# Retention and two matrix products on one core: states of the first six chunks as 64x64 blocks, and another order of the opening

## The chip, the cores and the metric

The kernel runs on one core of a Trainium2 chip. The metric is the time of one execution on the device in microseconds (us). A core has TensorE (PE in the profile; PEld is its weight load), VectorE (DVE), ScalarE (ACT), GpSimd (POOL) and SyncE (SP), which issues most of the transfers. Each engine has its own queue of instructions, works it off in order, and waits on semaphores for the others.

## The reference, cut to what matters

```python
def _attn_ref(q, k, v):                      # each 4 x 8 x 768 x 64
    gamma = 1.0 - 2.0 ** (-5.0 - np.arange(H))
    for t in range(S):
        state = gamma * state + k[:, :, t] (outer) v[:, :, t]     # 64 x 64 for each head
        y[:, :, t] = scale * q[:, :, t] @ state

def _moe_ref(x, w_in, w_out):                # x is 3072 x 512, made from y
    h = x @ w_in                             # 512 x 2048
    sp = np.where(h > 20.0, h, np.log1p(np.exp(np.minimum(h, 20.0))))
    return (h * np.tanh(sp)) @ w_out         # 2048 x 512
```

There are four batches, eight heads of width 64 and 768 steps in each sequence.

## The kernel before, in words

**Chunks.** The recurrence is done in chunks of 128 steps, six in a batch, 24 in all. For a chunk, the present part of y comes from scores (k times q, masked by a triangle with decay built into the scaled q and v), and the past part from the state at the end of the chunk before it (q times state). The state of a head is a 64x64 block: the sum of k-outer-v over the chunk (tile `u_ps`), plus the old state, times a decay factor for the chunk.

**How the states lie.** In chunks 0 to 4 of the first batch a pair of heads shares one full 128x128 matmul: k of two heads as weights, v of two heads as data. That gives a 128x128 block with the two wanted 64x64 blocks on its diagonal and two unwanted blocks beside them. So the state tile `st` is 128x4x128 (four pairs), and the factor tile `gcm` (L83, L105 to L108) is of that size, with the decay on the diagonal blocks and zeros elsewhere, so that one multiplication on DVE decays the state and clears the unwanted blocks (`state_first` L306, `decay_wide` L458). A past term (`past_first` L324, `past` L462) is then one full matmul for a pair of heads. From the second batch on the states are compact: 128x4x64 (`stc`), written by quarter or half-array matmuls (`outer` L425) and multiplied by the broadcast of a 128x4 tile (`gcv`).

**Blocks.** Rows of x are worked in blocks: the first of four chunks (512 rows, `first_block` L846), then blocks of two chunks. For each block, x times w_in goes to `h_ps`, through the activation on ACT, and then times w_out. Later blocks use a scheme with seven products instead of eight (`g1_seven`, `seven`). The order of all work on every engine is written out by hand: the program order is the order in each queue, and a wait on TensorE holds back whatever stands behind it.

**The opening** (`first_block`, L856 to L910). Its four chunks come as two sets of two chunks; in a set, a token pair lies in one partition, so that each half of the 64 partitions is one chunk. q is scaled on DVE, turned on TensorE and copied to `qfirst_t`. Each half (four heads) of k is cast to fp16 on ACT (`cast_two`, L248), turned by four transposes on TensorE (`turn_two`, L262) and copied from PSUM to SBUF on ACT (`turned_two`, L267). v is cast and scaled on POOL (L251). Scores are 64x64 quarter matmuls (L280), then masked on DVE (L287). The present terms are quarter matmuls too (L319). `spin` and `spin_wide` (L385, L390) are matmuls whose result is not used; the array is kept working with them. After the present and past terms of chunks 2 and 3, `xt_out` (L331) copies y to x, and `first_g1` (L842) begins x times w_in: 16 matmuls for chunks 0 and 1, then 16 for chunks 2 and 3. The state of chunk 3 (L299, L309 and L311 again) follows before the next group (L537).

**Chunks 4 and 5** are worked inside `first_g2` (L961), the second product of the first block. `outer_wide` (L448) makes the sum for chunk 4, adds the state of chunk 3, and `decay_wide` the decay; `y_two` (L511) makes the present and past terms of both chunks.

PSUM tiles come from two pools: tag `mm` has four buffers (turned halves, state sums, `h_ps`, `o_ps`), tag `at` two (scores, `y_ps`). A buffer is written again when its last reader has finished.

Of the kernel before, what the change touches and what calls it, by code (L numbers as in the profile page):

```python
# [16 lines left out]
def kernel(  # L17
# [9 lines left out]
    nc = tc.nc  # L27
# [52 lines left out]
    vs_two = qvs[:, (2 + CPB) * H:].rearrange("p (r h) -> p h r", r=R)  # L80
    ident = cpool.tile([P, P], FP16, name="ident")
    tri = cpool.tile([P, C], FP32, name="tri")
    gcm = cpool.tile([P, HP, P], FP32, name="gcm")  # L83
    gcv = cpool.tile([P, HP], FP32, name="gcv")
    warm = cpool.tile([P, 1], FP32, name="warm")
    gate_t = cpool.tile([P, 1], FP16, name="gate")
    nc.gpsimd.memset(ident, 0.0)
# [17 lines left out]
    nc.vector.memset(gcm, 0.0)  # L105
    for h in range(H):
        o = 64 * (h % 2)
        nc.vector.memset(gcm[o:o + 64, h // 2, o:o + 64], float(gamma[h] ** C))  # L108
        o = 64 * (h // HP)
        nc.vector.memset(gcv[o:o + 64, h % HP:h % HP + 1], float(gamma[h] ** C))  # L110
    decay = gcv.unsqueeze(2).broadcast_to((P, HP, D))

    win_ap = moe_w_in.rearrange("(bp p) f -> p bp f", p=P)
    wout_ap = moe_w_out.rearrange("(fb p) c -> p fb c", p=P)
# [4 lines left out]
    loaded, cast, qkts, ats, ams, states, us, ys, sus = {}, {}, {}, {}, {}, {}, {}, {}, {}  # L119
# [149 lines left out]
    def toks(c):  # L269
        return slice(c * HB, (c + 1) * HB)  # L270
# [19 lines left out]
            tri_first.rearrange("p r t -> p (r t)").unsqueeze(1).broadcast_to(  # L290
                (P, HP, R * C)), op=ALU.mult)

    def outer_first(s, chunks=(0, 1)):
        u_ps = {c: mmps.tile([P, HP, P], FP32, name="u_ps", tag="mm") for c in chunks}
        for i in range(HP):
            half, j = divmod(i, HP // 2)
            for r in range(R):
                for c in chunks:
                    nc.tensor.matmul(  # L299
                        u_ps[c][:, i], k16s[s][toks(c), half, r, 2 * j:2 * j + 2],  # L300
                        v16s[s, half][toks(c), r, 2 * j:2 * j + 2],
                        start=i == 0 and r == 0, stop=r == R - 1, skip_group_check=True)
        for c in chunks:
            us[2 * s + c] = u_ps[c]

    def state_first(g):  # L306
        u = us.pop(g)
        if g > 0:
            nc.tensor.matmul(u, ident, states[g - 1], start=False, stop=True, skip_group_check=True)  # L309
        states[g] = stp.tile([P, HP, P], FP16, name="st")  # L310
        nc.vector.tensor_tensor(states[g], u, gcm, op=ALU.mult)  # L311

    def present_first(s, y, pairs):
        for i in pairs:
            half, j = divmod(i, HP // 2)
            for r in range(R):
                for c in range(2):
                    for hh in range(2):
                        nc.tensor.matmul(  # L319
                            y[64 * hh:64 * hh + 64, c, i], v16s[s, half][toks(c), r, 2 * j + hh],  # L320
                            amf[s, half][toks(c), hh, j, r], start=i == 0 and r == 0,
                            stop=s == 0 and c == 0 and r == R - 1, skip_group_check=True)

    def past_first(g, y):  # L324
        for i in range(HP):
            nc.tensor.matmul(
                y[:, g % 2, i], states[g - 1][:, i], qfirst_t[:, i, g * C:(g + 1) * C],
                start=False, stop=True, skip_group_check=True)

    def xt_out(g, y):  # L330
        nc.scalar.copy(xts[0][:, g:g + 2], y)  # L331
# [113 lines left out]
            stcs[g] = stp.tile([P, HP, D], FP16, name="stc", tag="stc")  # L445
            by.tensor_tensor(stcs[g], sus.pop(g), decay, op=ALU.mult)

    def outer_wide(g):  # L448
        _, k16, v16, _ = cast[g]
        u_ps = u_tile()[:, 0]  # L450
        for i in range(HP):
            nc.tensor.matmul(
                u_ps[:, i], k16[:, 2 * i:2 * i + 2], v16[:, 2 * i:2 * i + 2],
                start=True, stop=True)
        sus[g] = stp.tile([P, HP, P], FP32, name="su", bufs=1)
        nc.vector.tensor_tensor(sus[g], u_ps, states[g - 1], op=ALU.add)

    def decay_wide(g):  # L458
        states[g] = stp.tile([P, HP, P], FP16, name="st")
        nc.vector.tensor_tensor(states[g], sus.pop(g), gcm, op=ALU.mult)  # L460

    def past(g, y):  # L462
        qt = qkts[g][0]
        if g < NCH:
            for i in range(HP):
                nc.tensor.matmul(
                    y(i), states[g - 1][:, i], qt[:, i], start=False, stop=True,
                    skip_group_check=True)
# [377 lines left out]
    def first_block():  # L846
        qf = load_first_q()
        for s in range(2):
            for nm in "kv":
                for half in range(2):  # L850
                    load_two(nm, s, half)
        nload[0] = CPB
        load_weights()
        xts[0] = xtp.tile([P, CPB, HP, C], FP16, name="xt")

        at = at_tile()  # L856
        spin_wide(at, HP)
        spin_wide(at, HP)
        spin(at, 8)
        tq = turn_first_q(qf, 0)  # L860
        spin_wide(at, 3)
        first_q_out(0, tq, nc.scalar)
        tq = [tq, turn_first_q(qf, 1)]
        cast_two("k", 0, 0)
        turn_two(0, 0)
        first_q_out(1, tq[1], nc.vector)
        turned_two(0, 0)
        cast_two("k", 0, 1)
        spin_wide(at, 3)
        scores_half(0, 0, at)  # L870
        mask_half(0, 0, at)
        turn_two(0, 1)
        turned_two(0, 1)
        for half in range(2):
            cast_two("v", 0, half)
        at = at_tile()
        spin_wide(at, 3)
        scores_half(0, 1, at)
        mask_half(0, 1, at)
        cast_two("k", 1, 0)  # L880
        turn_two(1, 0)
        turned_two(1, 0)
        cast_two("k", 1, 1)
        outer_first(0)
        state_first(0)
        at = at_tile()
        scores_half(1, 0, at)
        mask_half(1, 0, at)
        y = atps.tile([P, 2, HP, C], FP32, name="y_ps", tag="at")
        present_first(0, y, range(HP))  # L890
        turn_two(1, 1)
        turned_two(1, 1)
        state_first(1)
# [67 lines left out]
    def first_g2():  # L961
# [68 lines left out]
            mm(px[p], a(p, 1, 2), t(4))  # L1030
        for p in pairs:
            mm(px[p], a(p, 1, 1), b(1, 0))
        outer_wide(CPB)
        casts(CPB + 2)
        turn_by_dma(CPB + 2)
        load_q(CPB + 4)
        scores_one(CPB + 1)
        decay_wide(CPB)

        def end(p, i, half):  # L1040
            for f in range(2 * half, 2 * half + 2):
# [126 lines left out]
```

## Time and profile before

| what | value |
|---|---|
| median of three runs | 199.25 us (199.11 to 199.26) |
| profiled execution | 199.32 us |
| its span on the core | 197.5 us |
| busy: TensorE, DVE, ACT, POOL | 190.2, 142.5, 105.6, 92.9 us |
| state multiplies of the opening (L311) | four of 684 ns each |
| state matmuls of the opening (L299) | 32, 1.9 us busy |
| first block matmul (L842) | starts at 18.02 us |

The span runs from the first to the last instruction on the core; the rest of the time of an execution lies around it. A row of the timeline reads: start, duration, engine, source line, operation, output<-inputs, sizes, count; a count above one means that like instructions were merged. In square brackets stands how long the engine was idle before it and what ended that. Matmuls are pipelined: one starts while the one before it is still passing through the array, so the distance between starts tells the pace, and a duration holds some 0.2 us of latency. In the busy times by stretches the last three columns are the granted TensorE clock, the share of busy transfer engines and GB/s.

### The profile page before, as it was taken

To read this page: it belongs to the slowest core of one execution; us is meant where nothing else is said; L and a number is where in the kernel's file an instruction comes from. 1 tells how busy PE (TensorE), PEld (TensorE's weight loads), DVE (VectorE), ACT (ScalarE), POOL (GpSimd) and SP (SyncE) were. 2 spreads that over 40 slices of the span, in tenths; PEclk is the share of its full clock that TensorE was granted. 3 is DMA by queue.
4 is the path that set the end of the run, shared out by engine and by line. 5 is a ranking of instruction groups with operands and counts; after the bars stand their busy time and mean duration, and the time that the engine had idled before them with its cause. 6 is when DMAs were issued, how large, how long until landed. Compare 5 with 4: busy or idle time off the path is not lost.

```text
span 197.5 us, 5915 instructions
## 1 busy us (share of the span) xinstructions
PE 190.2 (96%) x2463; PEld 158.2 (80%) x2463; DVE 142.5 (72%) x295; ACT 105.6 (53%) x193; POOL 92.9 (47%) x129
## 2 busy tenths in 40 slices
PE   6899999999999999999999999999999999999992
PEld 2357646885988988988988988988988988988991
DVE  3687699788997596597498597597497596596462
ACT  3365667453663653753753753753753843843930
POOL 4063006596667739909716818818626723110000
PEclk9999999999999999999999999999999999999999
DMA  5999999999999999999999995996997954101102
GB/s 168 303 310 375 385 385 308 196 302 177 113 194 196 189 291 200 174 210 206 182 209 87 198 204 106 154 206 129 177 199 112 163 108 106 56 2 67 42 30 80
DMA packets 95802, 36.06 MB, mean 183 GB/s; under 512 B 82592, under 2 KB 89376, under 8 KB 95776
## 3 DMA queue, kind: packets, MB, share of 16 engines
q1 hardware_dynamic: 74544, 33.04, 74.2%
q0 software_dynamic: 21088, 2.62, 21.6%
q8 instruction: 19, 0.31, 0.6%
q14 instruction: 7, 0.06, 0.1%
q10 hardware_dynamic: 144, 0.03, 0.1%
HBM read 27.30 MB, written 6.29 MB: 170 GB/s over the span
## 4 chain that ended last, share of the span: by engine, by line
PE 91%; DMA 2%; DVE 2%; ACT 1%; issue 1%; DVEq 0%
PE o_ps L757 32%; PE h_ps L676 18%; PE h_ps L652 16%; PE h_ps L537 5%; PE o_ps L986 5%; PE y_ps L484 3%; PE at L414 3%; DMA qfirst<-in_q_dram 2%; PE o_ps L1042 2%; PE h_ps L842 2%; PE y_ps L475 1%; PE u_ps L429 1%; DVE am L287 1%; DVE st L311 1%; DVE qfirst L217 1%
## 5 line engine op out<-in xcount | busy, mean ns | idle before, releaser
L676 PE MATMUL h_ps<-xt,win 128*128 128x256 f16 x320 | 41.6, 273 | 0.0
L669 DVE TENSOR_TENSOR hsum<-h_ps,hsnap 128x512 f32<-128x512 f32 x30 | 19.8, 688 | 21.0 <-PE h_ps L652 18.9
L757 PEld LDWEIGHTS <-gsum 128*128 128x128 f16 x336 | 30.8, 98 | 4.2
L676 PEld LDWEIGHTS <-win 128*128 128x128 f16 x320 | 29.3, 98 | 3.6
L757 PE MATMUL o_ps<-tmat,gsum 128*128 128x256 f16 (+1 forms) x256 | 28.0, 266 | 0.0
L359 POOL DMA_DIRECT2D qk<-in_k_dram x36 | 27.8, 776 | 0.0
L757 PEld LDWEIGHTS <-g 128*128 128x128 f16 x256 | 23.7, 98 | 2.6
L663 ACT ACTIVATE g<-hsum 128x512 f16<-128x512 f32 x30 | 18.6, 630 | 11.5 <-DVE hsum L669 11.5
L420 DVE TENSOR_TENSOR am<-at,tri 128x1024 f16<-128x1024 f32 x20 | 24.3, 1215 | 0.0
L683 ACT ACTIVATE g<-h_ps 128x512 f16<-128x512 f32 x40 | 22.7, 599 | 2.4 <-PE h_ps L676 2.4
L364 POOL TENSOR_TENSOR v<-vf,qvs 128x512 f16<-128x512 f32 x20 | 23.6, 1178 | 0.0
L766 ACT COPY snap<-o_ps 128x256 f32<-128x256 f32 (+1 forms) x32 | 11.4, 359 | 21.6 <-PE o_ps L757 21.5
L659 ACT COPY hsnap<-h_ps 128x512 f32<-128x512 f32 x30 | 16.4, 580 | 11.5 <-PE h_ps L652 11.5
L372 POOL COPY gate<-gsum 128x1 f16<-128x1 f16 x12 | 2.6, 213 | 42.5 <-DVE gsum L723 36.8
L347 POOL TENSOR_TENSOR qk<-qf,qvs 128x512 f16<-128x512 f32 x20 | 21.7, 1085 | 1.3 <-DMA qf<-in_q_dram 1.3
L779 DVE TENSOR_TENSOR osb<-o_ps,snap 128x256 f32<-128x256 f32 (+1 forms) x31 | 12.7, 410 | 12.6 <-PE o_ps L757 11.4
L652 PEld LDWEIGHTS <-wsum 128*128 128x128 f16 x320 | 19.5, 98 | 0.5
L757 PE MATMUL o_ps<-wout,g 128*128 128x256 f16 (+1 forms) x168 | 19.3, 267 | 0.0
L522 ACT CAST xt<-y_ps 128x1024 f16<-128x1024 f32 x10 | 10.1, 1012 | 14.4 <-PE y_ps L475 14.4
L652 PE MATMUL h_ps<-xsum,wsum 128*128 128x128 f16 x240 | 16.7, 219 | 0.0
L652 PEld LDWEIGHTS <-win 128*128 128x128 f16 x240 | 15.1, 98 | 0.7 <-issue 0.2
L595 DVE TENSOR_TENSOR gsum<-g 128x256 f16<-128x256 f16 (+1 forms) x30 | 9.9, 331 | 3.8 <-ACT g L663 3.6
(121 smaller groups left out, 295.5 us busy)
## 6 DMA issues: line engine op xcount, KB each, us to landing
vf<-in_v_dram SPq DMA_DIRECT2D x24, 256.0 KB, 5.9
out_dram<-osb SPq DMA_DIRECT2D x22, 256.0 KB, 5.1
qf<-in_q_dram SPq DMA_DIRECT2D x20, 256.0 KB, 5.5
wi<-in_moe_w_in_dram SPq DMA_DIRECT2D x3, 1024.0 KB, 10.6
wt<-in_moe_w_out_dram SPq DMA_DIRECT2D x3, 1024.0 KB, 10.2
qk<-in_k_dram POOLq DMA_DIRECT2D x36, 64.0 KB, 4.8
qfirst<-in_q_dram SPq DMA_DIRECT2D x2, 512.0 KB, 5.4
kf<-in_k_dram SPq DMA_DIRECT2D x4, 256.0 KB, 6.1
```

What stands on the lines that cost most here:

```text
L347: nc.gpsimd.tensor_tensor(by_head(g, room16(g)[0]), by_head(0, loaded[g][0]), f.broadcast_to((P, 2, HP, D)), op=ALU.mult)
L359: nc.gpsimd.dma_start(room16(g)[1][:, x::2], src[:, HP * x:HP * x + HP])
L364: nc.gpsimd.tensor_tensor(room16(g)[2], loaded[g][2], vs.unsqueeze(2).broadcast_to((P, H, D)), op=ALU.mult)
L420: nc.vector.tensor_tensor(am, ats.pop(g), tri.unsqueeze(1).unsqueeze(1).broadcast_to((P, 2, HP, C)), op=ALU.mult)
L652: nc.tensor.matmul(h_ps[:, f], w(f, d), x(d), start=first and f == 0 and d == 0, stop=d == n - 1, skip_group_check=True)
L659: nc.scalar.copy(x, h_ps)
L663: nc.scalar.activation(gt[:, 2 * i * FPS:(2 * i + 1) * FPS, j * P:(j + 1) * P], h, AF.Mish, scale=inv_boost3)
L669: nc.vector.tensor_tensor(h, h_ps, x, op=ALU.add)
L676: nc.tensor.matmul(h_ps[:, j], win(s, 2 * half + j, bp), xt(blk, bp), start=bp == 0, stop=bp == NBP - 1)
L683: nc.scalar.activation(gt[:, fb:fb + 2], h_ps, AF.Mish, scale=inv_boost3)
L757: nc.tensor.matmul(t, x(f), w(f)[:, c], start=first and f == 0, stop=f == n - 1, skip_group_check=True)
L779: nc.vector.tensor_tensor(dst[:, c], t, plus[:, c], op=ALU.add)
```

## The change

The states of chunks 0 to 4 become compact tiles of 128x4x64 as in the later batches, though with the two heads of a pair in the two halves of the partitions. The sums are made by 64x64 quarter matmuls in the opening (`outer_first`), and by 128x64 half-array ones for chunk 4 (`outer_fifth`). The past terms of chunks 1 to 5 are pairs of quarter matmuls on the diagonal of the array. A small copy on ACT (`probe`) now reads y between the present and the past terms, and the past terms wait for it, because they write the same PSUM tile as that copy reads. In the opening, the second half of k of the first set is cast before the first half's turn is copied, and turned before the first scores; the state sums of chunks 0 and 1 move ahead of the turn of the second set; the spins are shorter; and four block matmuls of `first_g1` move ahead of the past terms of chunks 2 and 3. No transfer is added, taken away or moved.

```diff
-    gcm = cpool.tile([P, HP, P], FP32, name="gcm")
+    gcf = cpool.tile([P, HP], FP32, name="gcf")
+    probe = cpool.tile([P, R], FP32, name="probe")
...
-    def outer_first(s, chunks=(0, 1)):
-        u_ps = {c: mmps.tile([P, HP, P], FP32, name="u_ps", tag="mm") for c in chunks}
+    def outer_first(s, chunks=(0, 1), spins=0):
+        u_ps = {c: mmps.tile([P, HP, D], FP32, name="u_ps", tag="mm") for c in chunks}
+        for _ in range(spins):
+            nc.tensor.matmul(
+                u_ps[chunks[0]].rearrange("p i d -> p (i d)"), tri,
+                tri.unsqueeze(1).broadcast_to((P, R, C)), start=True, stop=True,
+                skip_group_check=True)
...
                 for c in chunks:
-                    nc.tensor.matmul(
-                        u_ps[c][:, i], k16s[s][toks(c), half, r, 2 * j:2 * j + 2],
-                        v16s[s, half][toks(c), r, 2 * j:2 * j + 2],
-                        start=i == 0 and r == 0, stop=r == R - 1, skip_group_check=True)
+                    for x in range(2):
+                        nc.tensor.matmul(
+                            u_ps[c][64 * x:64 * x + 64, i], k16s[s][toks(c), half, r, 2 * j + x],
+                            v16s[s, half][toks(c), r, 2 * j + x],
+                            start=i == 0 and r == 0, stop=r == R - 1, skip_group_check=True)
...
-            nc.tensor.matmul(u, ident, states[g - 1], start=False, stop=True, skip_group_check=True)
-        states[g] = stp.tile([P, HP, P], FP16, name="st")
-        nc.vector.tensor_tensor(states[g], u, gcm, op=ALU.mult)
+            nc.tensor.matmul(u, ident, stcs[g - 1], start=False, stop=True, skip_group_check=True)
+        stcs[g] = stp.tile([P, HP, D], FP16, name="stc", tag="stc")
+        nc.vector.tensor_tensor(stcs[g], u, decay_first, op=ALU.mult)
...
     def present_first(s, y, pairs):
...
+        nc.scalar.copy(probe, y[:, :, HP - 1, :1].rearrange("p c t -> p (c t)"))
 
     def past_first(g, y):
         for i in range(HP):
-            nc.tensor.matmul(
-                y[:, g % 2, i], states[g - 1][:, i], qfirst_t[:, i, g * C:(g + 1) * C],
-                start=False, stop=True, skip_group_check=True)
+            for x in range(2):
+                o = slice(64 * x, 64 * x + 64)
+                nc.tensor.matmul(
+                    y[o, g % 2, i], stcs[g - 1][o, i], qfirst_t[o, i, g * C:(g + 1) * C],
+                    start=False, stop=True, skip_group_check=True)
...
-    def outer_wide(g):
+    def outer_fifth(g):
...
-                u_ps[:, i], k16[:, 2 * i:2 * i + 2], v16[:, 2 * i:2 * i + 2],
-                start=True, stop=True)
-        sus[g] = stp.tile([P, HP, P], FP32, name="su", bufs=1)
-        nc.vector.tensor_tensor(sus[g], u_ps, states[g - 1], op=ALU.add)
...
+            for x in range(2):
+                nc.tensor.matmul(
+                    u_ps[64 * x:64 * x + 64, i], k16[:, 2 * i + x], v16[:, 2 * i + x],
+                    start=i == 0, stop=True, skip_group_check=True)
+        sus[g] = stp.tile([P, HP, D], FP32, name="suc", tag="suc")
+        nc.vector.tensor_tensor(sus[g], u_ps, stcs[g - 1], op=ALU.add)
...
     def past(g, y):
...
-                nc.tensor.matmul(
-                    y(i), states[g - 1][:, i], qt[:, i], start=False, stop=True,
-                    skip_group_check=True)
+                for x in range(2):
+                    o = slice(64 * x, 64 * x + 64)
+                    nc.tensor.matmul(
+                        y(i)[o], stcs[g - 1][o, i], qt[o, i], start=False, stop=True,
+                        skip_group_check=True)
...
         first_q_out(1, tq[1], nc.vector)
+        cast_two("k", 0, 1)
         turned_two(0, 0)
-        cast_two("k", 0, 1)
-        spin_wide(at, 3)
+        spin_wide(at, 1)
+        turn_two(0, 1)
+        turned_two(0, 1)
+        spin_wide(at, 1)
         scores_half(0, 0, at)
         mask_half(0, 0, at)
-        turn_two(0, 1)
-        turned_two(0, 1)
         for half in range(2):
             cast_two("v", 0, half)
         at = at_tile()
-        spin_wide(at, 3)
         scores_half(0, 1, at)
         mask_half(0, 1, at)
         cast_two("k", 1, 0)
+        outer_first(0, spins=1)
         turn_two(1, 0)
         turned_two(1, 0)
         cast_two("k", 1, 1)
-        outer_first(0)
         state_first(0)
...
         present_first(1, y, range(HP))
+        first_g1(h_ps[0], 0, 0)
         past_first(2, y)
         past_first(3, y)
         xt_out(2, y)
         cast_win(0, 1, nc.vector)
-        for u in range(FPS):
+        for u in range(1, FPS):
```

More of the change, by code (lines that the diff above doesn't have):

```diff
@@ L104 @@
     nc.scalar.activation(warm, warm, AF.Mish)
-    nc.vector.memset(gcm, 0.0)
     for h in range(H):
         o = 64 * (h % 2)
-        nc.vector.memset(gcm[o:o + 64, h // 2, o:o + 64], float(gamma[h] ** C))
+        nc.vector.memset(gcf[o:o + 64, h // 2:h // 2 + 1], float(gamma[h] ** C))
         o = 64 * (h // HP)
@@ L111 @@
     decay = gcv.unsqueeze(2).broadcast_to((P, HP, D))
+    decay_first = gcf.unsqueeze(2).broadcast_to((P, HP, D))
     win_ap = moe_w_in.rearrange("(bp p) f -> p bp f", p=P)
@@ L118 @@
     stcs = {}
-    loaded, cast, qkts, ats, ams, states, us, ys, sus = {}, {}, {}, {}, {}, {}, {}, {}, {}
+    loaded, cast, qkts, ats, ams, us, ys, sus = {}, {}, {}, {}, {}, {}, {}, {}
     xts, gts, wins, wouts, wtmps = {}, {}, {}, {}, {}
@@ L446, in state_decay, with decay_fifth @@
             by.tensor_tensor(stcs[g], sus.pop(g), decay, op=ALU.mult)
-    def outer_wide(g):
+    def outer_fifth(g):
         _, k16, v16, _ = cast[g]
-        u_ps = u_tile()[:, 0]
+        u_ps = u_tile()[:, 0, :, :D]
         for i in range(HP):
-            nc.tensor.matmul(
-                u_ps[:, i], k16[:, 2 * i:2 * i + 2], v16[:, 2 * i:2 * i + 2],
-                start=True, stop=True)
-        sus[g] = stp.tile([P, HP, P], FP32, name="su", bufs=1)
-        nc.vector.tensor_tensor(sus[g], u_ps, states[g - 1], op=ALU.add)
-    def decay_wide(g):
-        states[g] = stp.tile([P, HP, P], FP16, name="st")
-        nc.vector.tensor_tensor(states[g], sus.pop(g), gcm, op=ALU.mult)
+            for x in range(2):
[4 more added lines that the diff above has]
+        nc.vector.tensor_tensor(sus[g], u_ps, stcs[g - 1], op=ALU.add)
+    def decay_fifth(g):
+        stcs[g] = stp.tile([P, HP, D], FP16, name="stc", tag="stc")
+        nc.vector.tensor_tensor(stcs[g], sus.pop(g), decay_first, op=ALU.mult)
     def past(g, y):
@@ L465, in past @@
             for i in range(HP):
-                nc.tensor.matmul(
-                    y(i), states[g - 1][:, i], qt[:, i], start=False, stop=True,
-                    skip_group_check=True)
+                for x in range(2):
[3 more added lines that the diff above has]
+                        skip_group_check=True)
             return
@@ L1032, in first_g2 @@
             mm(px[p], a(p, 1, 1), b(1, 0))
-        outer_wide(CPB)
+        outer_fifth(CPB)
         casts(CPB + 2)
@@ L1037, in first_g2 @@
         scores_one(CPB + 1)
-        decay_wide(CPB)
+        decay_fifth(CPB)
         def end(p, i, half):
```

## The prediction

> **What bounds the kernel now.** I read the page first, then the busy time by stretches, then the timeline of the opening on TensorE, VectorE (DVE) and ScalarE (ACT), then narrow pieces of the same timeline for the price of one step. From the page, the share of TensorE and its slices:
>
> ```profile
> PE 190.2 (96%) x2463; PEld 158.2 (80%) x2463; DVE 142.5 (72%) x295; ACT 105.6 (53%) x193; POOL 92.9 (47%) x129
> PE   6899999999999999999999999999999999999992
> ```
>
> From the busy time by stretches (length, then busy time of each engine, its instructions in brackets):
>
> ```profile
> 14.00:18.00 4.00, 3.64 (x106) 2.62 (x95) 4.00 (x6) 1.52 (x3) 2.69 (x3) 1.00 1.07 365
> 18.00:22.00 4.00, 4.00 (x43) 3.44 (x41) 1.62 (x3) 2.61 (x5) 0.00 (x0) 1.00 1.05 388
> 22.00:50.00 28.00, 28.00 (x238) 18.05 (x235) 23.72 (x37) 15.21 (x26) 14.11 (x14) 1.00 1.29 281
> ```
>
> There are two regimes. Until about 18 us DVE is the full engine (4.00 of 4.00) and TensorE waits in places. From 18.0 us on TensorE is never idle. So what the change takes from TensorE's work after 18 us is gained in full, and before 18 us only an earlier start of the block matmuls (line 842) counts. The opening's timeline shows what sets that start:
>
> ```profile
> 10.37 0.42 PE L280 MATMUL at<-qfirst_t,qkt 64*64 64x128 f16 x16
> 11.81 0.62 ACT L248 CAST qk<-kf 128x512 f16<-128x512 f32 x1
> 12.92 0.58 ACT L267 COPY qkt<-t_ps 128x512 f16<-128x512 f16 x1 [0.49 <-PE t_ps L262]
> 13.56 0.42 PE L280 MATMUL at<-qfirst_t,qkt 64*64 64x128 f16 x16
> 14.17 1.22 DVE L287 TENSOR_TENSOR am<-at,tri_first 128x1024 f16<-128x1024 f32 x1
> 14.79 0.58 ACT L267 COPY qkt<-t_ps 128x512 f16<-128x512 f16 x1 [0.77 <-PE t_ps L262]
> 15.30 0.68 DVE L311 TENSOR_TENSOR st<-u_ps,gcm 128x512 f16<-128x512 f32 x1
> 15.91 1.23 DVE L287 TENSOR_TENSOR am<-at,tri_first 128x1024 f16<-128x1024 f32 x1
> 17.54 0.65 PE L326 MATMUL y_ps<-qfirst_t,st 128*128 128x128 f16 x8
> ```
>
> The columns are start, duration, engine, line. The last mask (15.91, ends 17.13) releases the second half of the present terms, then come the past terms at 17.54 and the blocks at 18.02. Two narrow pieces show what a change of tile shape on the array costs, and a quick form:
>
> ```profile
> 21.40 0.27 PE L842 MATMUL h_ps<-xt,win 128*128 128x256 f16 x1
> 21.61 0.23 PE L299 MATMUL u_ps<-v,qk 64*128 64x128 f16 x1
> 61.58 0.42 PE L429 MATMUL u_ps<-v,qk 128*64 128x64 f16 x16
> ```
>
> Full matmuls of 256 columns start 0.109 us apart (32 of L842 in 3.49), but from the last of them to the first half-array one it is 0.205: a change of shape costs 0.095. The pieces around 14.2, 17.5 and 22.1 us give the same 0.09 to 0.10. The last row: 16 matmuls in 128x64 tiles with 64 columns start within 0.42 less one latency of 0.20, eight pairs at 0.031 a pair. With 128 columns a pair takes 0.056 (L299: 16 in 0.62 less 0.22 at 12.81), and four 64x64 quarters side by side also 0.056 (L280: 16 in 0.42 less 0.22).
>
> **The change, part by part.** The sum is made against the profiled execution: 199.32 us, a span of 197.5 and 1.8 around it. The runs' median is 199.25, 0.07 lower.
>
> *Constants.* One memset of 0.48 us and eight of 0.11 become eight of 0.06. DVE is done with them at 2.8 us and waits until 5.77 for the first q. Nothing.
>
> *Turns and casts of k.* ACT now casts the second half of k ahead of the copy of the first turn. That half has landed by 9.0 us (issued at 2.33, landing within 6.7), so the cast runs 9.14 to 9.76 behind the first one. The copy still starts at 9.73, since it waits for the turn (9.30 and 0.40). The first scores stay at 10.37. The second turn and copy come at 9.82 and 10.24, the second scores at 10.88 instead of 11.96, and the second mask stands right behind the first, at 12.06 instead of 12.43. Next on this path is chunks 2 and 3: their k is issued at 5.86 and lands 5.8 us later, at 11.7, and its cast started at 11.81 already. It can move to 11.75 at most; turn, copy and scores follow as before (12.43, 12.87, 13.51), and their mask goes from 14.17 to 13.99, where DVE used to be late and now the scores are. The last scores wait for that mask's buffer (now free at 15.2) and for the copy of the last turn, 14.79 to 15.37 on ACT, which has moved by 0.06 at most. So the last mask moves from 15.91 to about 15.87: -0.04. The ends are -0.47 (were DVE alone the limit, below) and +0.05 (no gain, one more wait); I take the value nearest to the rows of ACT.
>
> *Moved up ahead of the turn of chunks 2 and 3:* the state matmuls. They wait for POOL's second cast of v (ends 12.14), and the turn waits behind them: quarters until 12.3 and a change of shape, 12.42, against a cast ready at about 12.43. No cost, with no room to spare. The spins in fp32 shrink from two of 384 columns to two of 128 and one of 256; they stand in waits either way.
>
> *States on DVE.* 0.68 becomes 0.42 (a multiply of 128x256 from PSUM in the groups by line: 415 ns). The first two end ahead of work that now waits for TensorE, and the third used to end at 17.73, when the second half of the past terms was waiting for it; that wait was 0.02. It is counted in the next part.
>
> *Probe.* A 128x2 copy on ACT, 0.2 us (between the 0.20 of a 128x1 activation and the 0.27 of a 128x128 copy). It waits for the last present matmul; behind it on ACT stand the copy of the last turn and the copy of x. The first probe runs at 14.4 to 14.6, ahead of a turn that ends at 14.75. The past terms wait for it, no sooner than 14.7. The second ends 0.5 us after the last present matmul starts, and the moved-up block matmul covers that (next). If that cover were gone the past terms would wait 0.3.
>
> *One of the block's matmul groups ahead of the past terms.* From the last present matmul to the state matmuls of chunk 3 (21.61) it was 4.22 us: 0.15, eight past matmuls at 0.056, 32 block matmuls at 0.109, a change. Now: 0.15, four block matmuls (0.44), a change, sixteen quarters, a change, 28 block matmuls (3.06), a change. The quarters lie on the array's diagonal, and no row shows that pattern. If a pair runs side by side, eight pairs take 0.45 as the eight full ones did; if not, 0.89. I take 0.45, as all other pairs in different rows of the array do it. That makes 4.37: +0.15, two changes of shape less the wait. The copy of x (1.01) is done 0.14 before its readers come.
>
> *State matmuls of chunk 3, all on the path:* eight at 0.056, a change, and the old state by 512 columns until 22.39, 0.78 in all. Now eight pairs at 0.031 and a change, 0.34, and 256 columns, 0.12: 0.46. That is -0.31. At 0.056 a pair it would be -0.12.
>
> *Fifth chunk.* Four full matmuls (0.22) and one change become four pairs at 0.031 (0.12) and two changes: -0.02. The past terms of chunks 4 and 5: as many array steps, and one change more (+0.09). The next block starts at 49.37 because the copy of x ends at 49.32 (48.31 and 1.01), while TensorE was ready at 49.32 too; the new change is seen by 0.04 past that. DVE's halved sum and decay (0.69 and 1.01 before) are off the path.
>
> Sum: -0.04 +0.15 -0.31 -0.02 +0.04 = -0.18, so 199.14 against 199.32, and 199.07 against the median. I say 199.1. The later waits do not eat it: the two halves of the last quarter of the output weights land at 42.1 and 43.6 and are cast by 43.2 and 44.7 for readers at 44.4 and 46.1, and the turn of chunk 4 at 38.89 hangs on POOL's cast, which follows DVE and ACT work that moves with TensorE.
>
> **Rivals.** *Quarters one after the other (slower).* The two past stages would take 0.45 more each: 199.14 + 0.89 = 200.0. For: in before, matmuls in different rows of the array always write different 2 KB halves of their PSUM tile (scores by half-head, present terms by chunk), while the diagonal quarters write one half. Against: they write different partitions of it. It decides from 0.067 us a pair, where the sum is zero. [...]
>
> *DVE's queue was the limit (faster).* Four masks 1.13 apart and two states of 0.34 would follow each other from 10.91, the last mask ending 0.9 earlier. POOL's cast of the first weights ends at 17.01, which caps the gain at 0.47: 198.7. Against: the ACT rows above.
>
> *The state matmuls do not get quicker* (0.056 a pair): 199.34, no change. A pair in one half of the rows, unlike the 128-row pairs of the row shown, has no row in the trace.
>
> *The clock (slower).* With half a microsecond less spinning, TensorE could fall back to the pace of the first microseconds, where two 512-column fp16 matmuls start 0.43 apart against 0.22 later. That lasted some 5 us (1.87 to 7.05), so up to 2.6 lost: 201.7. Against: I expect no pause above 0.8 us. [...]
>
> **How the numbers follow.** Forecast 0.57, quarters apart 0.13, DVE 0.11, no quicker states 0.14, clock 0.05. A difference of 0.2%, 0.4 us, is about what a measurement of this kernel can tell from none. The forecast's own range is 198.8 to 199.4, and 0.05 of it lies below 198.85; another 0.03 lies above 199.65 for small waits that I have not seen. Faster 0.16, same 0.63, slower 0.21. The range goes from 198.6 (the DVE case) to 200.1 (quarters apart); outside is the clock.
>
> **What would show it.** Right: last mask near 15.87, eight past quarters a pair at 0.056, the states of chunk 3 in 0.46 from the first to the next block, block matmuls again without pause. Wrong: past quarters over 0.9 us for sixteen; half-pace matmuls after 10 us; the last mask under 15.5; a wait of the past terms for the probe.

## The result, and the profile after

The changed kernel takes 201.7 us (median of 19 runs, 200.04 to 203.36), the kernel before on the same chip 199.24 (19 runs). The ratio is 1.011, with a 95% interval of 1.009 to 1.013: slower, where no change was forecast. The profiled execution shown here took 203.16 us, a span of 201.4. The runs of the changed kernel stand in three groups by their mean granted clock, 200.0 to 200.3 us at 0.999 or 1.0, 201.5 to 202.1 at 0.990 or 0.991 and 202.9 to 203.4 at 0.983, and the ratio leaves out three of the last group, among them the profiled one.

From the page of the changed kernel, TensorE's total, its slices and the slices of its granted clock:

```profile
PE 192.6 (96%) x2521; PEld 160.1 (80%) x2521; DVE 140.2 (70%) x294; ACT 106.0 (53%) x195; POOL 92.4 (46%) x129
PE   6986999999999999999999999999999999999992
PEclk9997599999999999999999999999999999999999
```

TensorE is busy for 2.4 us more although its work was to shrink, and the clock is down in the fourth and fifth slice (15 to 25 us). The busy time by stretches has the place (length; busy time of PE, PEld, DVE, ACT, POOL with counts; granted clock, transfer share, GB/s). The first three rows are of the changed kernel in the same stretches as those shown of the kernel before; the last three divide the time anew:

```profile
14.00:18.00 4.00, 2.40 (x73) 1.64 (x70) 3.33 (x5) 1.66 (x3) 2.12 (x3) 0.99 1.07 364
18.00:22.00 4.00, 3.47 (x35) 2.28 (x35) 1.21 (x2) 1.15 (x2) 0.00 (x0) 0.50 1.04 387
22.00:50.00 28.00, 28.00 (x225) 18.62 (x224) 20.43 (x33) 15.34 (x27) 11.92 (x13) 0.95 1.20 274
...
16.80:18.50 1.70, 0.27 (x7) 0.11 (x7) 0.85 (x2) 0.00 (x0) 0.00 (x0) 0.82 1.03 377
18.50:24.70 6.20, 6.17 (x47) 4.20 (x47) 1.29 (x2) 1.34 (x3) 0.00 (x0) 0.50 1.05 386
24.70:50.00 25.30, 25.30 (x213) 16.70 (x211) 20.34 (x32) 15.15 (x26) 11.92 (x13) 1.00 1.22 263
```

Two things are new: 1.7 us in which TensorE hardly works, and 6.2 us in which it works at half clock. From 24.7 on everything is as before. Rows of the timeline of the same stretch, DVE and ACT included (start, duration, engine, line; in brackets the idle time and what ended it):

```profile
10.80 2.35 DVE L288 TENSOR_TENSOR am<-at,tri_first 128x1024 f16<-128x1024 f32 x2 [0.74 <-PE at L281]
14.07 0.16 ACT L330 COPY probe<-y_ps 128x2 f32<-128x2 f32 x1 [0.45 <-PE y_ps L326]
14.39 0.41 PE L336 MATMUL y_ps<-qfirst_t,stc 64*64 64x128 f16 x8
15.49 1.23 DVE L288 TENSOR_TENSOR am<-at,tri_first 128x1024 f16<-128x1024 f32 x1 [0.32 <-PE at L281]
16.77 0.30 PE L326 MATMUL y_ps<-am,v 64*64 64x128 f16 x7 [0.42 <-DVE am L288]
18.53 0.48 PE L326 MATMUL y_ps<-am,v 64*64 64x128 f16 x9 [1.46 <-issue]
18.94 1.03 PE L855 MATMUL h_ps<-xt,win 128*128 128x256 f16 x4
19.91 1.06 PE L336 MATMUL y_ps<-qfirst_t,stc 64*64 64x128 f16 x16
20.90 5.08 PE L855 MATMUL h_ps<-xt,win 128*128 128x256 f16 x28
25.91 0.44 PE L306 MATMUL u_ps<-v,qk 64*64 64x64 f16 x16
26.40 1.89 PE L550 MATMUL h_ps<-xt,win 128*128 128x512 f16 x8
```

The same stretch of the kernel before, from its present terms to the next group:

```profile
16.66 0.94 PE L319 MATMUL y_ps<-am,v 64*64 64x128 f16 x32
18.02 3.66 PE L842 MATMUL h_ps<-xt,win 128*128 128x256 f16 x32
22.39 4.91 PE L537 MATMUL h_ps<-xt,win 128*128 128x512 f16 x22
```

The opening reaches its last mask within 0.2 us of the forecast, counted from q's landing. In this execution q landed 0.57 us earlier than in the one shown of before, so the last mask starts at 15.49 instead of 15.91. But the sixteen present matmuls that this mask releases are torn in two: seven start at 16.77, nine at 18.53, with 1.46 us idle in between that nothing explains but "issue". No semaphore, engine or transfer of data ends it; the waits of TensorE have it as a row of their own:

```profile
PE y_ps L326 <- issue: 1.5, 1, 1.5
```

After the pause the 28 block matmuls take 5.08 us, 0.18 for one, where 32 took 3.66 before. The next group of matmuls starts 10.91 us after the start of the last mask, 6.48 before. Of those 4.4 us the pause is 1.6 (from 16.86, the last start ahead of it, to 18.53, less one step of 0.056), and half the pace for 6.2 us is 3.1. The rest, -0.3, is only what is left over; the forecast for this stretch was -0.16 (+0.15 and -0.31). From that group to the end it is 175.0 us, before 175.1.

### The profile page after: what moved, and what is told of

Read it like the earlier page. It is cut to its first block, busy times and chain, and to the rows that moved or that the text cites. A ratio compares the mean times of both kernels' runs of the same rounds, so it can differ in the third digit from the quotient of the medians.

```text
span 201.4 us, 6034 instructions
## 1 busy us (share of the span) xinstructions
PE 192.6 (96%) x2521; PEld 160.1 (80%) x2521; DVE 140.2 (70%) x294; ACT 106.0 (53%) x195; POOL 92.4 (46%) x129
## 4 chain that ended last, share of the span: by engine, by line
PE 94%; DVE 2%; issue 1%; ACT 1%; POOL 0%; POOLq 0%; DVEq 0%
PE o_ps L770 31%; PE h_ps L689 18%; PE h_ps L665 16%; PE h_ps L550 5%; PE o_ps L1000 5%; PE h_ps L855 3%; PE y_ps L497 3%; PE at L424 3%; PE at L400 2%; PE o_ps L1056 2%; DVE am L288 1%; PE y_ps L488 1%; PE u_ps L439 1%; PE at L281 1%; PE y_ps L326 1%
## 5 line engine op out<-in xcount | busy, mean ns | idle before, releaser
L696 ACT ACTIVATE g<-h_ps 128x512 f16<-128x512 f32 x40 | 22.8, 599 | 2.4 <-PE h_ps L689 2.4
L792 DVE TENSOR_TENSOR osb<-o_ps,snap 128x256 f32<-128x256 f32 (+1 forms) x31 | 12.7, 410 | 12.5 <-PE o_ps L770 11.4
L535 ACT CAST xt<-y_ps 128x1024 f16<-128x1024 f32 x10 | 10.1, 1012 | 14.4 <-PE y_ps L488 14.3
L566 ACT ACTIVATE g<-h_ps 128x512 f16<-128x512 f32 x16 | 9.3, 598 | 6.2 <-PE h_ps L550 3.7
```

The source lines that it names most:

```text
L696: nc.scalar.activation(gt[:, fb:fb + 2], h_ps, AF.Mish, scale=inv_boost3)
L792: nc.vector.tensor_tensor(dst[:, c], t, plus[:, c], op=ALU.add)
```

## The experiments

Three theories were to be told apart for the pause. The code theory: TensorE reaches an instruction that has not been brought yet, since the change puts more instructions ahead of it. The spin theory: the shorter spins of the opening let the clock fall. The third: the new order or the compact states cost time by themselves. For the code theory the page has a row in its list of queues, with packets, MB and share of time:

```profile
q8 instruction: 19, 0.31, 0.7%
```

0.31 MB in 19 packets is 16 KB each. One of them goes from 16.00 to 17.13 us, and 1.4 us after its end TensorE goes on. Counting TensorE's instructions up to the pause from the trace (matmuls and weight loads, the two counts in brackets after the PE and PEld times) gives 223 + 224 = 447:

```profile
0.00:18.50 18.50, 13.45 (x223) 7.98 (x224) 10.65 (x28) 8.00 (x13) 7.41 (x16) 0.98 0.97 282
```

In the kernel before, instruction 447 is one of the block matmuls and runs at 19.33, which comes after a packet from 16.77 to 17.82. The count up to 19.30 in the kernel before is 445:

```profile
0.00:19.30 19.30, 15.89 (x222) 9.02 (x223) 12.35 (x29) 8.84 (x13) 7.39 (x16) 1.00 0.98 287
```

In the changed kernel it is a present matmul, since 60 more instructions lie ahead of the end of the present terms (464 against 404): 48 of them in the state sums and 8 in the first past terms, where two quarters stand for one wider matmul, each with its weight load; the rest are spins.

**The same number of instructions without the change.** The kernel before, with 28 small matmuls (56 instructions) added at the spins of the opening, where TensorE waits for q in any case:

```diff
+    def pad(at, n):
+        for _ in range(n):
+            for hh in range(2):
+                for x in range(2):
+                    o = slice(64 * hh, 64 * hh + 64)
+                    nc.tensor.matmul(
+                        at[64 * x:64 * x + 64, hh, 0, 0, :64], ident[o, :64], ident[o, :64],
+                        start=True, stop=True, skip_group_check=True)
...
         spin(at, 8)
+        pad(at, 7)
```

> The kernel before, with 28 small 64x64 matmuls (56 instructions with their weight loads, results not used) added behind the first spins, where TensorE waits for q from 6.1 to 7.0 us. Nothing else is changed. Code theory (TensorE's next block of 256 instructions arrives late, and the changed kernel stops where that block begins): the same place now lies 56 instructions earlier in the work, inside the present and past terms of chunks 2 and 3, so a pause of 0.8 to 1.8 us with no releaser appears there between 16.7 and 19 us, and the time goes from 199.2 to 200.0 or more, with the half pace of the array behind it in some executions (up to 203). Spin theory (the shorter spins let the clock fall, and the pause belongs to that): nothing was taken from the spins, so 199.2, no pause.

Measured: 200.82 us against 199.0, ratio 1.009 (1.006 to 1.012). The timeline, and then the count up to 18.5 us:

```profile
16.56 0.85 PE L319 MATMUL y_ps<-am,v 64*64 64x128 f16 x25
18.54 0.30 PE L319 MATMUL y_ps<-am,v 64*64 64x128 f16 x7 [1.13 <-issue]
```

```profile
0.00:18.50 18.50, 14.38 (x223) 7.89 (x224) 12.35 (x29) 7.83 (x12) 7.41 (x16) 1.00 0.99 284
```

The kernel before, with nothing changed but this, pauses behind the same 447 instructions, in its own present matmuls. Its clock is 1.00 in every stretch from 10 to 50 us (10 to 18, 18 to 19, 19 to 23, 23 to 50), so 1.3 us (from start to start) is the price of the pause alone. The profiled execution loses another 0.6 at 51.4 us, where TensorE waits for ACT's copy of x; what delays that copy was not followed up.

**The parts of the change one by one.** First the changed kernel with the old length of the two spins ahead of the first scores:

```diff
-        spin_wide(at, 1)
+        spin_wide(at, 3)
...
-        spin_wide(at, 1)
+        spin_wide(at, 3)
```

> The changed kernel with the two short spins of the opening back at 384 columns each, as they were before (the count of instructions stays the same). Code theory: nothing changes, 200.0 to 203.4 with the pause of about 1.5 us in the second half of the present terms of chunks 2 and 3. Spin theory: the clock stays at 1.00 throughout and the time falls to 199.0 to 199.3.

Then the kernel before with the changed kernel's order of the opening and its spins, on wide states (so with the 16 full sums in place of 32 quarters):

```diff
         first_q_out(1, tq[1], nc.vector)
+        cast_two("k", 0, 1)
         turned_two(0, 0)
-        cast_two("k", 0, 1)
-        spin_wide(at, 3)
+        spin_wide(at, 1)
+        turn_two(0, 1)
+        turned_two(0, 1)
+        spin_wide(at, 1)
         scores_half(0, 0, at)
...
         cast_two("k", 1, 0)
+        outer_first(0, spins=1)
```

> The kernel before with the new order of the opening alone, short spins included: states of 128x128, past terms as before, no probe, block matmuls where they were. Code theory: the count of instructions ahead of the present terms is within 4 of the kernel before, so the place falls into the block matmuls as before, 199.1 to 199.3 and a clock of 1.00. Spin theory: the clock falls as in the changed kernel, 200.5 to 203.4.

And the changed kernel with the old order and spins of the opening (the same lines the other way):

> The changed kernel with the opening in the order and with the spins of the kernel before; states as 64x64 blocks, quarter past terms, probe and the moved block matmuls kept. Code theory: the pause is there as in the changed kernel, 200.0 to 203.4. Spin theory: no pause and a clock of 1.00, 199.0 to 199.3.

Measured: long spins 201.2 us (1.013, 1.006 to 1.020), with a pause of 1.36 us and a clock of 0.57 from 19 to 23 us; order alone 199.1 (0.999, 0.997 to 1.002), no pause, clock 1.00 from 10 to 50 us; states alone 202.31 (1.018, 1.013 to 1.024), with a pause of 1.94. So the order and the short spins cost nothing that this measurement can tell (0.997 to 1.002). The loss comes with the rest of the change, in which the quarter matmuls add the instructions, and the two that pause do so behind 447 instructions (223 + 224), as the changed kernel does.

**Moving the place.** In the changed kernel one wide spin gives way to 80 (or 92) small matmuls, so that instruction 447 comes some 156 (or 180) earlier in the work, where TensorE waits anyway:

```diff
         spin_wide(at, HP)
-        spin_wide(at, HP)
+        pad(at, 20)
```

> The changed kernel with one wide spin at the start replaced by 80 small 64x64 matmuls whose results are not used: 156 more instructions ahead of the opening. [...] If a block takes no more than 6.6 us from request to use, no pause is left at the present terms of chunks 2 and 3, the clock stays at 1.00 and the time is 199.0 to 199.3; if the first one is still late, a pause of up to 1 us stands near 13.7 us and the time is 199.3 to 200.2. Were the pause one of the work itself (the second half of the present terms waiting for something not in the records), it stays at that place: 200.0 to 203.4.

> As the kernel with 80 small matmuls, with 92: 180 more instructions. Code theory: first block boundary at about 13.5 us, asked for at about 6 us; second at about 19.6 us, asked for at 13.5, which is 6.1 us: a pause of 0 to 0.6 us in the block matmuls, 199.0 to 199.7. Otherwise as there.

When TensorE asks for a packet no run shows; the times of a request in the expectations are estimates of the author's.

Measured: with 80 more, 199.33 us (1.003, 1.000 to 1.005), with 92 more, 200.76 (1.008, 1.005 to 1.011). The first, in the stretch where the changed kernel pauses:

```profile
16.76 0.64 PE L326 MATMUL y_ps<-am,v 64*64 64x128 f16 x32
17.65 0.61 PE L864 MATMUL h_ps<-xt,win 128*128 128x256 f16 x4 [0.25 <-POOL win L183]
18.20 0.63 PE L336 MATMUL y_ps<-qfirst_t,stc 64*64 64x128 f16 x16
```

More instructions in all, and the loss is gone in the median; one of its ten runs still took 201.56 us at a mean clock of 0.983, and why stays open. The queue of instructions has 20 packets with 80 more (0.33 MB on the page), and 19 in the kernel before and in the changed one. With twelve matmuls more the loss is back in part, above the 199.7 us expected at most, and the timeline and the count show where:

```profile
20.38 1.80 PE L864 MATMUL h_ps<-xt,win 128*128 128x256 f16 x15 [0.22 <-issue]
```

```profile
0.00:20.30 20.30, 15.43 (x351) 9.73 (x352) 10.77 (x28) 9.16 (x15) 7.43 (x16) 1.00 0.97 292
```

351 + 352 = 703, which is 256 more than 447, and again "issue" is all that ends the idle time. That costs 0.4 us (0.49 between starts instead of 0.11), which is not all of the loss. The present terms, which start at 16.76 and run through with 80 more, come in two halves here, at 16.71 and, after a wait of 0.42 for the last mask, at 17.55; what delays that mask was not followed up.

**Taking instructions away.** A kernel with the compact states and the new order, and 64 instructions fewer. It leaves out one token of each pair in the state sums and the present terms of chunks 0 and 1; the loop of the present terms is changed like that of the sums:

```diff
-            for r in range(R):
+            for r in range(R - (s == 0)):
...
-                            start=i == 0 and r == 0, stop=r == R - 1, skip_group_check=True)
+                            start=i == 0 and r == 0, stop=r == R - 1 - (s == 0),
+                            skip_group_check=True)
```

> The changed kernel without half of two sums of chunks 0 and 1: their states and present terms take one token of each pair (r = 0) alone, so 32 matmuls and their weight loads, 64 instructions, are left out ahead of the present terms of chunks 2 and 3. These matmuls lie in waits for ScalarE and VectorE, so the chain of the opening keeps its length. Code theory: the block boundary moves into the block matmuls, as in the kernel before; the pause goes, the clock stays at 1.00, 198.9 to 199.3 (what my forecast said of the change alone). If the pause belongs to the work at its place, it stays: 200.0 to 203.4.

Measured: 198.85 us, 0.998 (0.997 to 0.999), clock 1.0. Its timeline:

```profile
17.20 0.61 PE L856 MATMUL h_ps<-xt,win 128*128 128x256 f16 x4
17.75 0.63 PE L337 MATMUL y_ps<-qfirst_t,stc 64*64 64x128 f16 x16
18.31 0.50 PE L856 MATMUL h_ps<-xt,win 128*128 128x256 f16 x3
19.04 1.14 PE L856 MATMUL h_ps<-xt,win 128*128 128x256 f16 x9 [0.23 <-issue]
```

Instruction 447 is now a block matmul, and only a remnant of the pause is left (0.23 idle, 0.50 between starts instead of 0.11). So the change almost without the pause is 0.3 us quicker than the kernel before, with the reservation that this kernel also does less work.

**Why the packet comes so late.** In the changed kernel the transfers are full: the share of their time is over 1.0 in every stretch shown that begins at 14 us or later. Two attempts to hold back the loads of weights until the packet was through did not hold them: in the first, 315 GB/s were moved from 12 to 14 us, as in the changed kernel, and in the second the first load that was to wait was issued at 11.52 us, against 11.13 there.

> The changed kernel, with the loads of all weights but the first quarter of w_in held back on SyncE until ScalarE has cast the last k (about 13.6 us in place of 11.2), by one 256-byte transfer that waits for that buffer. The transfers already issued last until about 16.9 us, so nothing lands much later. Backlog theory (the block of instructions is late because it stands behind the data transfers already issued): fewer transfers stand ahead of it, its transfer begins before 16.0 us and the pause shrinks by as much, down to none: 199.0 to 200.0. If it is late for another reason (asked for late, or as slow as any transfer while the engines are full): it begins at 15.7 to 16.8 us as in all five profiles so far, and the time is 200.0 to 203.4.

Measured: 201.54 us (1.012, 1.007 to 1.017), pause 1.39.

> The changed kernel, in which the loads of the second part of w_in and everything behind them on SP are issued only after the last cast of k on ACT (a transfer of 64 values into the buffer that this cast frees stands in front of them), so from about 13.6 us instead of 11.1. Backlog theory (the third block of 256 TensorE instructions comes late because its transfer queues behind those of the weights): that block is brought before 15.5 us instead of at 16.0, the pause in front of TensorE's 447th instruction falls below 0.6 us or vanishes, the clock stays at 1.0 and the time is below 200.0 us if the weights themselves are not late. Request theory (it is asked for at a fixed point of the instruction stream and takes its time whatever else is moved): the packet starts within 0.3 us of 16.0, the pause stays at 1.1 to 1.9 us and the time at 200.0 to 203.4 us.

Measured: 201.37 us (1.014, 1.010 to 1.018), packet at 15.60, pause 1.45; the transfer in front passed at 10.87 us, before the last cast of k had begun (12.50). Both say nothing for or against. The third reads what the last cast of k has written, and so does wait for it:

```diff
+    hold = cpool.tile([1, D], FP16, name="hold")
...
-        load_weights()
...
         cast_two("k", 1, 1)
+        nc.sync.dma_start(hold, k16s[1][:1, 1, 0, 0])
+        load_weights()
```

> The changed kernel, in which all loads of weights wait on SP until the last cast of k on ACT has ended (about 13.1 us; a transfer of 64 values that this cast wrote stands in front of them), so that by 13.6 us nothing but TensorE's instructions is left to move. Backlog theory: the third block of 256 TensorE instructions, asked for near 12 us, no longer queues behind the weights; its packet starts by 14.5 us instead of at 16.0, and TensorE does not pause in front of its 447th instruction while the clock stays at 1.0 up to there. Request theory (it takes its 4 us from the request whatever else is moved): the packet starts within 0.4 us of 16.0 and the pause stays at 1.1 us or more. By both the weights themselves come some 3 us later, so that waits for them can keep the time above 200 us; the time decides nothing here, the packet and the pause do.

Measured: the last cast of k ended at 13.09, and from 13.1 to 14.3 us no data moved, as meant; 202.19 us (1.016, 1.013 to 1.019). First the transfers of the changed kernel from 12.5 to 15.5 us and from 15.9 to 17.2 (busy tenths, then the queues), and below them those of this kernel from 12.5 to 14.5:

```profile
DMA  9999999999999999999999999999999999999999
q1 hardware_dynamic: 1105, 1.01, 110.8%
...
q1 hardware_dynamic: 244, 0.47, 100.5%
q8 instruction: 1, 0.02, 5.4%
```

```profile
DMA  9987894000000000000000000000000000000010
q1 hardware_dynamic: 170, 0.07, 14.7%
q8 instruction: 1, 0.02, 3.7%
```

In the changed kernel 1.01 MB of data go by from 12.5 to 15.5 us, and the packet of instructions only after them; with the weights held it goes at 12.76 instead of 16.00. A packet that took a fixed time from its request, the rival in the expectation, would have stayed near 16.0. The timeline of the kernel with held weights:

```profile
16.24 0.42 PE L327 MATMUL y_ps<-am,v 64*64 64x128 f16 x16 [0.41 <-DVE am L289]
18.77 0.92 PE L856 MATMUL h_ps<-xt,win 128*128 128x256 f16 x4 [2.11 <-POOL win L184]
19.62 1.06 PE L337 MATMUL y_ps<-qfirst_t,stc 64*64 64x128 f16 x16
```

The sixteen present matmuls run through, instruction 447 (at 16.32) among them. The pause for code is gone. The price has another name now, 2.11 us for the weights that were held back, and the clock falls after it all the same (0.50 from 20 to 22 us). So the packet is late because it shares the transfers with the weights, as far as one profiled execution shows it.

**Compact states without more instructions ahead.** Only the state of chunk 3 and what follows it become compact; up to the block matmuls the kernel is the one before:

```diff
+    def state_third():
+        u = mmps.tile([P, HP, D], FP32, name="u_ps", tag="mm")
...
+                    nc.tensor.matmul(
+                        u[64 * x:64 * x + 64, i], k16s[1][toks(1), half, r, 2 * j + x],
+                        v16s[1, half][toks(1), r, 2 * j + x],
+                        start=i == 0 and r == 0, stop=False, skip_group_check=True)
+        for x in range(2):
+            o = slice(64 * x, 64 * x + 64)
+            nc.tensor.matmul(
+                u[o], ident[:, o], states[2][:, :, o], start=False, stop=True,
+                skip_group_check=True)
+        stcs[3] = stp.tile([P, HP, D], FP16, name="stc", tag="stc")
+        nc.vector.tensor_tensor(stcs[3], u, decay_first, op=ALU.mult)
...
-                outer_first(1, [1])
-                state_first(3)
+                state_third()
```

> The kernel before, in which only the state of chunk 3 and what follows it (the fifth chunk's sum and decay, the past terms of chunks 4 and 5) are compact; nothing is changed ahead of the block matmuls, and the old state of chunk 2 is added by two half-array matmuls of 256 columns. Code theory: no instruction is added ahead of the 449th, so there is no pause and no drop of the clock; the state matmuls of chunk 3 take 0.46 us instead of 0.78 as in the changed kernel, and the time is 0.2 to 0.4 us under the kernel before: 198.8 to 199.1, faster than both. If the loss lay in the compact states themselves (their quarter matmuls or the past terms of the later chunks), the time would be above 199.5.

> As the run with compact states from chunk 3 on, with the changed kernel's order of the opening (turns and casts of k, states of chunks 0 and 1 earlier, shorter spins) on wide states. Code theory: the order adds hardly an instruction, so again no pause and a clock of 1.0; the order alone was worth 0.1 us within its error, so 198.7 to 199.1.

Measured: 198.02 us against 198.97, ratio 0.995 (0.994 to 0.997), with the old order; 198.52, 0.997 (0.995 to 0.998), with the new one. Both beat both kernels, by more than expected (198.8 to 199.1 and 198.7 to 199.1). The first one's stretch from the block matmuls to the next group:

```profile
16.91 3.66 PE L866 MATMUL h_ps<-xt,win 128*128 128x256 f16 x32
20.49 0.44 PE L315 MATMUL u_ps<-v,qk 64*64 64x64 f16 x16
20.86 0.30 PE L321 MATMUL u_ps<-st,ident 128*64 128x256 f16 x2
21.09 6.22 PE L561 MATMUL h_ps<-xt,win 128*128 128x512 f16 x28
```

No pause; the state of chunk 3 takes 0.60 (20.49 to 21.09) instead of 0.78, where 0.46 was expected. From there to the end it is 175.1 us, as before. So 0.18 us of the gain is shown. The other 1.1 us by which the profiled span of 196.2 is shorter come from q, which landed at 4.56 instead of 5.67 in these two executions. Landings of 4.73 (order alone) and 5.10 (the changed kernel) lie between these, with nothing changed in that load; whether this kernel's q comes earlier as a rule, or its runs were lucky, stays open.

## Why the prediction was wrong

*The failed step* is the one that counts the instructions of the opening. "The change, part by part" priced the state sums and past terms by their time on the array: pairs at 0.031 and 0.056 us, changes of shape at 0.095. It took the number of instructions for free. The 60 more ahead of the end of the present terms move the 447th instruction from the block matmuls, where it runs at 19.33 us, into the present terms, where it runs at 16.86, while the packet ends at 17.82 in the one kernel and at 17.13 in the other. The sum has no term for the wait; it measures 1.1 to 1.9 us of idle time, and the 28 small matmuls in the kernel before show it without anything else of the change. What it does to the clock comes on top: half-pace matmuls after 10 us (0.18 for one of 256 columns against 0.109), which the prediction had named as a sign of being wrong.

*"I expect no pause above 0.8 us"* fell with it. It is what the prediction sets against the clock, to which it gave 0.05. The rival named 201.7 us, which is the measured median, but that is luck, since it comes by another sum: it put 2.6 us on a slow pace after less spinning, while the profiled execution has 1.6 us of pause and 3.1 of half pace, at a mean clock of 0.983. The shorter spins, which it blamed, have no part in it: with them in the kernel before the clock stayed at 1.00 from 10 to 50 us, and with the long ones in the changed kernel it fell to 0.57 from 19 to 23. The slow pace came with a pause instead: the changed kernel's is 1.46 us long, and the clock fell (last section).

*Quarters one after the other* is refuted. Eight past quarters took 0.41 us less 0.22, four pairs at 0.05 to 0.06 us, and with no pause or slow clock about them sixteen took 0.56 from start to start with a change of shape (17.75 to 18.31 in the kernel with less work), as forecast (0.45 and 0.095).

*The state of chunk 3* measured 0.49 (25.91 to 26.40) against 0.46 forecast, so "the state matmuls do not get quicker" falls as well.

*The order of the opening* was put at -0.04. From q's landing to the last mask it is 10.24 us before, 10.28 with the order alone and 10.39 in the changed kernel, so +0.04 and +0.15; the order alone measures 0.999 with 1.0 in its interval. Its first scores did not stay put, though: they start 5.16 after q's landing, 4.70 before, since the second turn stands ahead of them. "DVE's queue was the limit" is out.

*The probe* takes 0.16 us and no past term waits for it, as forecast.

Without the pause the forecast's -0.18 is not contradicted: 199.33 us with the place moved and 198.85 with less work lie on either side of the 199.18 that the kernel before took on that chip. It is not shown either.

## What to carry to other kernels

Where a change adds many small matmuls, count TensorE's instructions ahead of the work that must not stop, not only their time (60 more here, and a pause of 1.46 us), and look at when the packets of its instructions arrive while the transfers are full (16.00 to 17.13 us here, at a share of over 1.0). An idle time that ends with "issue", at the same count of instructions in different kernels (447 here), is the sign. What helped here was fewer instructions ahead of that place (198.85 us with 64 fewer), or a place that falls into a wait or into long matmuls (199.33 with 80 small matmuls more at the start).

## What the runs showed of the hardware

The queue of instructions (q8) brings packets of 16 KB, 19 in the changed kernel and 20 with 80 matmuls more on TensorE. They share the transfers with the data: the packet ahead of the end of the pause came at 16.00 us, and at 12.76 with the weights held back. In the changed kernel it took another 1.4 us from that packet's end to TensorE's next instruction (17.13 to 18.53); in the kernel before, which does not pause, instruction 447 runs 1.5 us after the packet's end (17.82 to 19.33). That this packet holds the instructions behind the pause is read from the counts and the times; no row says what a packet holds.

TensorE's clock fell from 1.00 to 0.50 at 17.90 us in the changed kernel, although the longest idle time of TensorE after its start is 1.46 us, and it was back at 24.73. The changed kernel and the one with 28 matmuls more, in stretches of 3.41 us about their pauses:

```profile
14.49:17.90 3.41, 1.91 (x64) 1.31 (x64) 2.84 (x5) 1.40 (x2) 1.63 (x2) 1.00 1.07 365
17.90:21.31 3.41, 2.78 (x32) 1.77 (x32) 0.52 (x1) 0.46 (x2) 0.00 (x0) 0.50 1.04 386
21.31:24.73 3.42, 3.42 (x18) 2.44 (x17) 0.78 (x2) 0.91 (x2) 0.00 (x0) 0.50 1.05 385
24.73:28.14 3.41, 3.41 (x37) 2.11 (x36) 1.54 (x3) 2.57 (x5) 0.00 (x0) 1.00 1.04 386
```

```profile
17.20:20.61 3.41, 2.28 (x37) 1.92 (x33) 1.03 (x2) 1.01 (x1) 0.00 (x0) 1.00 1.05 387
```

In the changed kernel the stretch in which the pause begins has 1.91 us of busy time, and the clock is 0.50 in the next one; that one has 2.78, and the clock is 0.50 again; after the third, which is busy throughout, it is 1.00. In the other kernel the stretch with the pause has 2.28, and the clock was 1.00 behind it too (23 to 50 us). So a pause of 1.46 us came with 3.1 us of half pace and one of 1.13 with none; how busy TensorE has to be to keep its clock, these two executions do not show.
